# An earlier third second-stage call in a Fourier-mixing and cosine-MLP kernel, and one weight row over another queue

## The chip, the cores and the metric

The kernel runs on one core of a Trainium2 chip. The metric is the time of one execution on the device in microseconds (us); the kernel before has a median of 1911.01 us over three runs (1909.88 to 1911.72). Engines are named as in the profile: PE is TensorE's matmuls and PEld its weight loads, DVE is VectorE, ACT is ScalarE, POOL is GpSimd, SP is SyncE, which here only issues DMAs.

## The reference

```python
def _attn_ref(x):                      # x: 8 x 3008 x 256, float32
    X = np.fft.fft(x, axis=1)
    X = np.fft.fft(X, axis=2)
    return X.real.astype(np.float32)

def _moe_ref(x, w_in, w_out):          # 256 x 2048 and 2048 x 256
    h = x @ w_in
    g = h * np.cos(h)
    return (g @ w_out).astype(np.float32)
# the 24064 x 256 rows of the first are the x of the second
```

## The kernel before

The transform over the sequence is split as 3008 = 47 x 64. A **first stage** folds the input (x plus and minus its mirror) and multiplies it by cosines and sines of the 47; its result z goes to DRAM (`zd<-zs`) and comes back turned (`z<-zd`). A **second stage** multiplies z by the table `BJ` and gives `pq`, the input of the matmuls with `w_in`. The transform over the 256 columns is folded into `w_in` beforehand: `WC` and `WS` are the folded weights, and one row of each, `nrow`, is kept aside as a norm row. It has 2048 values, in four quarters of 512.

The main work is a list of 384 **steps**: 8 batches, 6 groups of sequence columns each (225 columns in group 0, 256 in the others), 8 steps a group. So batch b has the steps 48b to 48b+47. One step makes 2 x 128 hidden units for one group:

- `seed` (ACT, L734) writes the norm row's part, nb times a column of `wn`, into a PSUM tile H;
- `mm1(cur, 0)` (PE, L764, `WC`), `act_e` (ACT, L775), `mm1(cur, 1)` (PE, `WS`), `dve_h` (DVE, L780) make H and its partner h;
- `act_round` (ACT, L795), `dve_frac` (DVE, L799), `act_sin` (ACT, L805), `dve_g` (DVE, L809) make the cosine's argument, its sine and the product, once for H and once for h;
- `dve_s` (DVE, L820 and L830) makes sums S, and `mm2` (PE, L855) multiplies by `w_out` and its sums `VX`, adding into PSUM tiles M over the 8 steps of a group.

The steps are pipelined by hand in one loop. In pass t, PE does mm1 of step t and mm2 of step t-3; DVE does h of step t, the fractions of step t-1, g and S of step t-2 and the last S of step t-3; ACT seeds step t+1. After a group, ACT takes M (`take_m`, L876), GpSimd combines it (L907), DVE transposes it (L957) and SP stores it.

The next batch's transform runs beside the steps, in places that are written out as offsets. `transform(b)` counts from t0 = 48(b-1), the first step of the batch before. It puts loads of x, folds on GpSimd (`fold_rows`, L339; `fold_ends`, L351) and on DVE (`fold_pair`, `fold_edge`, L364) into passes, and **sessions** into the dictionary `sessions`: a session is a call whose matmuls stand between mm1(cur, 0) and mm2 of a pass. First-stage sessions (L396) are at t0 + 12, 20, 28 and 36. Second-stage sessions (`later_pair`, products L537) take two groups each: call 0 at t0 + 44, call 1 at t0 + 54, call 2 at t0 + 62. Their results go into a PSUM bank (`pb`) and into the H tile that step t+1 will use; ACT copies both into `pq` (`take_pair`, L584), and SP sends one row to DRAM and spreads it over the partitions as nb (L587, L588). Call 2 serves groups 4 and 5, whose first step is t0 + 80.

Batch 0 has its first stage and its groups 0 and 1 in an opening of its own; its calls 1 and 2 are at steps 14 and 22, and are needed at steps 16 and 32. The opening writes the queues out by hand: SP issues, in this order, the third quarter's columns of the norm row, a part of BJ, `send_row(3)` (the last quarter of the norm row to DRAM, `wd<-nrow`, L689), `take_columns(3)` (back as columns of `wn`, `wn<-wd`, L692, 512 elements of 4 bytes), `load_z(0, 1)` (L523), two loads of `w_out` (`load_w2`, L254), and then batch 1's x. GpSimd's queue has stores of z, four adds, three memsets, and then 14 loads of batch 1's x (L182) and two of its ends (L191); after them stand GpSimd's sums of `w_out` for the last four eighths (L907) and the first `fold_rows`. The last quarter of `wn` is first read by the seed of step 6, in pass 5.

In the loop the order around a session is:

```python
        if session:
            dve_g(old, 0)
            session[0](*session[2:], step(t + 1))
        if done and t > LAG:
            mm2(done, 0)
        if session:
            session[1](*session[2:], 1, step(t + 1).H)
```

Of the kernel before, what the change touches and what calls it, by code (L numbers as in the profile page):

```python
# [136 lines left out]
def kernel(  # L137
# [7 lines left out]
    nc = tc.nc  # L145
# [143 lines left out]
    nrow = {}  # L289
# [227 lines left out]
    def load_z(b, far):  # L517
        if b not in z2s:
            z2s[b] = spool.tile([128, NJ * 128], FP, tag="z2", bufs=1, name="z2")
        cols = slice(128 * JA, None) if far else slice(0, 128 * JA)  # L520
        zv = zds[b, far].rearrange("(x e r) c -> e x r c", e=2, r=2)
        for e in range(2):
            ins = nc.sync.dma_start(out=z2s[b][64 * e : 64 * e + 64, cols], in_=zv[e])  # L523
        return ins
# [83 lines left out]
    def transform(b):  # L608
        t0 = (b - 1) * NG * 8

        def at(o, *call):
            todo.setdefault(max(t0 + o, LAG - 1), []).append(call)

        for p, o in enumerate((0, 13) if b == 1 else (-20, -9)):
            for k in range(4):
                at(0 if o == 0 else o + k, load_later_x, b, p, k % 2, k // 2)
        at(0 if b == 1 else -16, load_ends, b)
        for c in range(NCH):
            o = 7 + 8 * (c // 2) + 2 * (c % 2)
            for e in range(2):  # L620
                aside.setdefault(t0 + o + e, []).append((fold_rows, b, c, e))
                between.setdefault(t0 + o + e + 1, []).append((fold_pair, c, e))
        for k in range(NCH // 2):
            o = 12 + 8 * k
            sessions[t0 + o] = first_half_later, take_half, b, k
            at(o, take_first, b, k)
            at(o + 1, store_z, b, k, 0)
            at(o + 1, store_z, b, k, 1)
        for e in range(2):
            o, f = (9 + e, 11) if b == 1 else (8 * e - 3, 6 + e)  # L630
            aside.setdefault(t0 + o, []).append((fold_ends, e))
            between.setdefault(t0 + f, []).append((fold_edge, e))
        at(38, load_z, b, 0)
        at(38, load_z, b, 1)
        later_pair(t0 + 44, b, 0)
        later_pair(t0 + 54, b, 1)
        later_pair(t0 + 62, b, 2)

    def later_pair(t, b, k):
        sessions[t] = second_pair, take_pair, b, k  # L640
        todo.setdefault(t, []).append((take_plus, b, k))
# [32 lines left out]
    def keep_row(e, n, pw, _):  # L674
        if n > 1:
            nrow[n] = half_tile("nrow", n)
        nc.vector.tensor_copy(out=nrow[n][0:1, :], in_=pw[0:1, :])
# [6 lines left out]

    wds = {}

    def send_row(n):
        wds[n] = dpool.tile([1, 512], FP, tag="wd", bufs=4, name="wd")
        nc.sync.dma_start(out=wds[n], in_=nrow[n][0:1, :])  # L689

    def take_columns(n):
        nc.sync.dma_start(  # L692
            out=wn[:, 4 * n : 4 * n + 4], in_=wds[n].rearrange("o (q p) -> (o p) q", p=128)
        )

# [326 lines left out]
    for row in range(2):  # L1022
        send_row(row)
    load_w2(0, 2)
    load_w2(2, 4)
    send_row(2)
    for k, c in enumerate(order[4:]):
        store_z(0, c, 1)
        if k:
            take_columns((1, 2, 0)[k - 1])  # L1030
# [11 lines left out]
        for dst, a, b, less in w2_sums:  # L1042
            aside.setdefault(f - 1, []).append((add, dst[:, f], a[:, f], b[:, f], less))
    n = len(steps)
    later_pair(14, 0, 1)
    later_pair(22, 0, 2)
    for b in range(1, NB):
        transform(b)

# [8 lines left out]
    clear_later(dve_h(s0))  # L1058
    late = fold_weights(1, 3, units=(1,), pw=late[2])
    keep_row(*late)  # L1060
    send_row(3)
    take_columns(3)
    load_z(0, 1)
    load_w2(4, 6)
    load_w2(6, 8)
# [136 lines left out]
```

## Time and profile before

| | |
|---|---|
| median of three runs | 1911.01 us |
| the profiled execution's own time | 1911.12 us |
| its span, first to last instruction | 1909.3 us |
| granted TensorE clock, mean | 0.999 |
| PE busy | 1894.7 us (99%) |
| DVE busy | 1781.9 us (93%) |
| ACT busy | 1489.5 us (78%) |
| POOL busy | 413.9 us (22%) |
| chain that ended last, by engine | PE 95%, DMA 2%, DVE 1% |

Times in a timeline count from the span's start. "Busy" is a union of an engine's instructions; matmuls are pipelined, so the end of one overlaps the start of the next. What stands in brackets at the end of a row is the idle time ahead of it and what ended it. A wait row reads: engine and line that waited, what it waited for, us in total, how often, the longest.

### The profile page before, as it was taken

What the parts mean: (1) busy time and instruction counts of PE and PEld (TensorE: products, weight loads), DVE (VectorE), ACT (ScalarE), POOL (GpSimd) and SP (SyncE); (2) the same over time, 40 slices, a digit from 0 to 9 for tenths busy, and PEclk for the clock granted to TensorE, in tenths of its full rate; (3) what the DMA queues carried; (4) which work ended last, traced back from release to release, by engine and by line L of the source; (5) the groups of instructions that cost most, each with busy time, mean ns of one, the idle gap of its engine ahead of it and who ended that gap; (6) DMA issues with size and microseconds to landing.
All of it is one profiled execution on the core that took longest, in us unless ns stands there. A gap on an engine that the chain in (4) does not pass through costs nothing.

```text
span 1909.3 us, 31666 instructions
## 1 busy us (share of the span) xinstructions
PE 1894.7 (99%) x10486; PEld 1664.4 (87%) x10486; DVE 1781.9 (93%) x3340; ACT 1489.5 (78%) x2682; POOL 413.9 (22%) x493
## 2 busy tenths in 40 slices
PE   8999999999999999999999999999999999999998
PEld 5888898888988889888898888988889888898887
DVE  7999999999999999999999999999999999999998
ACT  4777887778777887778877878778777877787775
POOL 5322112221122211222122221122211222111111
PEclk9999999999999999999999999999999999999999
DMA  7321311113111131111311113111231001200001
GB/s 221 79 56 44 72 51 26 30 47 74 42 33 28 50 75 35 35 32 45 80 33 32 28 46 91 27 26 28 54 86 26 24 20 29 59 20 16 13 22 23
DMA packets 154132, 88.61 MB, mean 46 GB/s; under 512 B 106207, under 2 KB 146058, under 8 KB 151629
## 3 DMA queue, kind: packets, MB, share of 16 engines
q1 hardware_dynamic: 150561, 82.80, 17.9%
q0 software_dynamic: 1376, 1.84, 0.4%
q10 hardware_dynamic: 2032, 1.95, 0.3%
q8 instruction: 83, 1.36, 0.3%
q14 instruction: 80, 0.66, 0.1%
HBM read 49.27 MB, written 37.28 MB: 45 GB/s over the span
## 4 chain that ended last, share of the span: by engine, by line
PE 95%; DMA 2%; DVE 1%; POOL 0%; issue 0%; ACT 0%; SPq 0%; ACTq 0%; DVEq 0%; POOLq 0%
PE M L855 59%; PE H L764 33%; PE pz L396 1%; PE pb L537 1%; DMA z<-zd 1%; DMA xp<-in_x_dram 0%; DVE S L820 0%; DVE r L809 0%; POOL zd L513 0%; PE pz L459 0%; PE H L537 0%; DVE S L830 0%; PE H L396 0%; DMA out_dram<-ob 0%; DVE xp L214 0%
## 5 line engine op out<-in xcount | busy, mean ns | idle before, releaser
L855 PE MATMUL M<-S,VX 128*128 128x256 f32 (+1 forms) x2304 | 612.3, 375 | 0.0
L855 PEld LDWEIGHTS M<-S,VX 128*128 128x128 f32 x2304 | 437.7, 190 | 50.0
L795 ACT ACTIVATE r<-H 128x512 f32<-128x512 f32 (+1 forms) x384 | 226.3, 589 | 284.9 <-DVE h L780 282.4
L805 ACT ACTIVATE r<-r 128x1024 f32<-128x1024 f32 (+1 forms) x384 | 395.9, 1031 | 28.8 <-DVE r L799 21.3
L855 PE MATMUL M<-r,w 128*128 128x256 f32 (+1 forms) x1536 | 393.4, 378 | 0.0
L764 PE MATMUL H<-pq,WS 128*128 128x256 f32 (+1 forms) x1536 | 388.0, 375 | 1.2 <-ACT ew L775 1.2
L764 PE MATMUL H<-pq,WC 128*128 128x256 f32 (+1 forms) x1536 | 387.7, 375 | 0.0
L734 ACT ACTIVATE H<-nb,wn 128x256 f32<-128x256 f32 (+1 forms) x762 | 362.0, 475 | 14.0
L780 DVE TENSOR_TENSOR h<-ew,H 128x512 f32<-128x512 f32 (+1 forms) x384 | 259.2, 675 | 90.3 <-PE H L764 72.0
L764 PEld LDWEIGHTS H<-pq,WS 128*128 128x128 f32 x1536 | 291.5, 190 | 35.8 <-ACT ew L775 2.9
L855 PEld LDWEIGHTS M<-r,w 128*128 128x128 f32 x1536 | 296.1, 196 | 27.4
L764 PEld LDWEIGHTS H<-pq,WC 128*128 128x128 f32 x1536 | 291.6, 190 | 31.2
L799 DVE SCALAR_TENSOR_TENSOR r<-r,H 128x512 f32<-128x512 f32 (+1 forms) x384 | 258.8, 674 | 18.3
L820 DVE TENSOR_TENSOR S<-r 128x512 f32<-128x512 f32 (+1 forms) x384 | 260.9, 679 | 0.1
L907 POOL TENSOR_TENSOR cb<-cb,mr 128x256 f32<-128x256 f32 (+3 forms) x190 | 159.2, 849 | 465.9 <-DVE S L830 313.5
L799 DVE SCALAR_TENSOR_TENSOR r<-r,h 128x512 f32<-128x512 f32 (+1 forms) x384 | 259.5, 676 | 0.0
L775 ACT ACTIVATE ew<-H 128x512 f32<-128x512 f32 (+1 forms) x384 | 225.9, 588 | 42.5 <-PE H L764 37.8
L809 DVE SCALAR_TENSOR_TENSOR r<-h,r 128x512 f32<-128x512 f32 (+1 forms) x384 | 258.5, 673 | 0.0
L809 DVE SCALAR_TENSOR_TENSOR r<-H,r 128x512 f32<-128x512 f32 (+1 forms) x384 | 256.7, 669 | 0.7 <-ACT r L805 0.2
L795 ACT ACTIVATE r<-h 128x512 f32<-128x512 f32 (+1 forms) x384 | 235.7, 614 | 0.0
L339 POOL TENSOR_TENSOR xs<-xp 113x512 f32<-113x512 f32 x112 | 143.0, 1277 | 419.1 <-DVE S L830 303.9
L855 PE MATMUL M<-S,w 128*128 128x256 f32 (+1 forms) x768 | 228.9, 380 | 2.9 <-DVE S L830 2.6
(113 smaller groups left out, 1534.5 us busy)
## 6 DMA issues: line engine op xcount, KB each, us to landing
out_dram<-ob SPq DMA_DIRECT2D x726, 32.0 KB
xp<-in_x_dram SPq DMA_DIRECT2D x256, 56.0 KB
z<-zd SPq DMA_DIRECT2D x16, 640.0 KB
zd<-zs SPq DMA_DIRECT2D x120, 80.0 KB
nb<-nd SPq DMA_DIRECT2D x23, 256.0 KB
xp<-in_x_dram SPq DMA_DIRECT2D x52, 48.0 KB
xp<-in_x_dram SPq DMA_DIRECT2D x42, 49.0 KB
z<-zd SPq DMA_DIRECT2D x16, 128.0 KB
```

What stands on the lines that cost most here:

```text
L339: return nc.gpsimd.tensor_tensor(out=rows_of(c, e)[0:XL], in0=xv[:, 0], in1=xv[:, 1], op=ALU.subtract if e else ALU.add,)
L734: nc.scalar.activation(out=s.H[:, u * T : u * T + T], in_=s.nb[:, 0:T], func=AF.Copy, bias=0.25, scale=wn[:, f : f + 1],)
L764: nc.tensor.matmul(s.H[:, u * T : u * T + T], lhsT=W[:, 128 * f : 128 * f + 128], rhs=s.pq[e][:, 0:T], start=False, stop=True, skip_group_ ...
L775: nc.scalar.mul(out=s.ew[:, 0 : 2 * s.T], in_=s.H[:, 0 : 2 * s.T], mul=2.0)
L780: return nc.vector.tensor_tensor(out=s.h[:, 0 : 2 * T].rearrange("p (u t) -> p u t", u=2)[:, :, ::-1], in0=s.ew[:, 0 : 2 * T].rearrange("p ...
L795: nc.scalar.activation(out=r, in_=h, func=AF.Copy, bias=BIG, scale=1.0)
L799: nc.vector.scalar_tensor_tensor(out=r, in0=r, scalar=-BIG, in1=h, op0=ALU.add, op1=ALU.subtract)
L805: nc.scalar.activation(out=r, in_=r, func=AF.Sin, bias=0.0, scale=SIN_SCALE)
L809: nc.vector.scalar_tensor_tensor(out=r, in0=h, scalar=-0.25, in1=r, op0=ALU.add, op1=ALU.mult)
L820: return nc.vector.tensor_tensor(out=sv[:, 0:2], in0=gv[:, 2:3].to_broadcast([128, 2, T]), in1=gv[:, 0:4:3], op=ALU.subtract,)
L855: nc.tensor.matmul(acc[key][m // 2][:, 256 * (m % 2) : 256 * (m % 2) + T], lhsT=w, rhs=a, start=first, stop=s.fp == 7, skip_group_check=True,)
L907: return nc.gpsimd.tensor_tensor(out=o, in0=a, in1=b, op=ALU.subtract if less else ALU.add)
```

## The change

Three edits. In every batch from 1 on, call 2 of the second stage goes from t0 + 62 to t0 + 57, which is from step 14 to step 9 of the batch itself, counted from its own first step. In batch 0, calls 1 and 2 go from steps 14 and 22 to steps 9 and 14. And the last quarter of the norm row and its columns are issued on GpSimd's queue instead of SP's; they stand there behind the memsets of `clear_later` and ahead of GpSimd's loads of batch 1's x. The number of instructions of each kind on TensorE, VectorE and ScalarE stays; two DMAs change their queue.

```diff
@@ transform(b)
         later_pair(t0 + 44, b, 0)
         later_pair(t0 + 54, b, 1)
-        later_pair(t0 + 62, b, 2)
+        later_pair(t0 + 57, b, 2)
@@
-    def send_row(n):
+    def send_row(n, queue=nc.sync):
         wds[n] = dpool.tile([1, 512], FP, tag="wd", bufs=4, name="wd")
-        nc.sync.dma_start(out=wds[n], in_=nrow[n][0:1, :])
-
-    def take_columns(n):
-        nc.sync.dma_start(
+        queue.dma_start(out=wds[n], in_=nrow[n][0:1, :])
+
+    def take_columns(n, queue=nc.sync):
+        queue.dma_start(
             out=wn[:, 4 * n : 4 * n + 4], in_=wds[n].rearrange("o (q p) -> (o p) q", p=128)
         )
@@
-    later_pair(14, 0, 1)
-    later_pair(22, 0, 2)
+    later_pair(9, 0, 1)
+    later_pair(14, 0, 2)
@@
     keep_row(*late)
-    send_row(3)
-    take_columns(3)
+    send_row(3, nc.gpsimd)
+    take_columns(3, nc.gpsimd)
     load_z(0, 1)
```

## The prediction

> **What bounds the kernel now.** I read the engine table first, then the length of every step in the TensorE timeline, then the waits of a stretch in which steps are long, then that stretch in the DVE and ACT timelines, and last the opening on the SP and POOL queues.
>
> ```profile
> PE 1894.7 (99%) x10486; PEld 1664.4 (87%) x10486; DVE 1781.9 (93%) x3340; ACT 1489.5 (78%) x2682; POOL 413.9 (22%) x493
> ```
>
> TensorE is the bound. A step lasts from its first `H<-pq,WC` matmul to the next one's; most full steps last 4.75 us, first-stage or second-stage calls included 6.04. So 99% can only shrink where a step is longer than its matmuls. I number steps within a batch, 0 to 47; step 57 of the diff is step 9 of a batch, 62 is 14. Steps 8 to 11 last 4.62, 4.56, 4.70 and 4.87 us in batch 3 (begun at 767.82, 772.44, 777.00, 781.70, ended 786.57) and the same within 0.01 in batches 2 to 6; in batch 7, which folds no next batch, they last 4.39, 4.39, 4.39 and 4.75 (from 1701.88). The matmuls are the same, so 0.23, 0.17, 0.30 and 0.13 us are stalls. The waits of batch 3's stretch 763.6 to 793 name them; batch 7's stretch has no such row:
>
> ```profile
> PEld M L855 <- DVE S L830: 0.9, 3, 0.4
> ```
>
> The three timelines of step 10 (start, us):
>
> ```profile
> 780.25 0.93 PE L855 MATMUL M<-S,VX 128*128 128x225 f32 x4
> 781.21 0.66 PE L855 MATMUL M<-S,w 128*128 128x225 f32 x2
> 781.70 1.03 PE L764 MATMUL H<-pq,WC 128*128 128x256 f32 x4
> ```
> ```profile
> 776.67 0.68 DVE L780 TENSOR_TENSOR h<-ew,H 128x512 f32<-128x512 f32 x1
> 777.27 0.69 DVE L809 SCALAR_TENSOR_TENSOR r<-H,r 128x512 f32<-128x512 f32 x1
> 778.02 0.69 DVE L799 SCALAR_TENSOR_TENSOR r<-r,H 128x512 f32<-128x512 f32 x1
> ...
> 780.43 0.42 DVE L364 TENSOR_TENSOR xf<-xs 113x254 f32<-113x254 f32 x1
> 780.76 0.39 DVE L830 TENSOR_TENSOR S<-r,S 128x225 f32<-128x225 f32 x1
> ...
> 781.40 0.69 DVE L780 TENSOR_TENSOR h<-ew,H 128x512 f32<-128x512 f32 x1
> ```
> ```profile
> 777.39 0.60 ACT L795 ACTIVATE r<-H 128x512 f32<-128x512 f32 x1 [1.02 <-DVE h L780]
> 782.12 0.60 ACT L795 ACTIVATE r<-H 128x512 f32<-128x512 f32 x1 [0.15 <-DVE h L780]
> ```
>
> DVE goes from one h (776.67) to the next (781.40) in 4.73 us without a pause, against 4.39 of matmuls: the fold (L364, 0.33 of it) is what batch 7 lacks. The last matmul pair waits for S of 780.76 and starts at 781.21, 0.05 us behind its end, where it could have started at 781.01. ACT rounds only once h is done, and DVE's L799 waits for that rounding: h, rounding, L799 is the loop.
>
> In the opening:
>
> ```profile
> 36.99 0.24 SPq L689 DMA_DIRECT2D wd<-nrow  x1
> 39.60 0.36 SPq L692 DMA_DIRECT2D wn<-wd  x1
> 40.18 1.24 SPq L523 DMA_DIRECT2D z<-zd  x2
> ```
> ```profile
> 53.96 0.27 PE L537 MATMUL M<-BJ,z 64*64 64x64 f32 x1 [0.28 <-DMA z<-zd]
> ```
> ```profile
> 67.16 1.70 DVE L820 TENSOR_TENSOR S<-r 128x450 f32<-128x450 f32 x1
> ```
>
> SP sits 2.3 us between the row and its columns, with z behind them, and TensorE later waits for z. The third line is an op that takes 0.62 us elsewhere: GpSimd's fold (66.99, 1.38 us) runs beside it.
>
> **Part 1, batches 1 to 7, third call from step 14 to 9.** Removed and added alike: 64 products on TensorE, two ACT copies (0.59, 0.58), two DMAs. A call lengthens a step by 1.30 us (6.05 against 4.75 at 14; 5.48 against 4.19 at 6), so TensorE's own sum is unchanged. What changes is when DVE gets 1.30 us to catch up. Walking batch 3 on, in us from a step's start: step 9 now needs 4.39+1.30 = 5.69. Its products need L809 on H, done at 0.89; the call at 14, which waits for nothing, starts its products at 0.96, so no new wait (at most 0.05). h must now wait for the longer step: 4.82 instead of 4.24. That is 0.87 before step 10, earlier 0.33: DVE gains 0.54. ACT's rounding starts at -0.15, L799 at 0.48 instead of 1.02; S for the last pair is ready at 3.61 instead of 4.15, the pair starts at 4.01 unhindered, and the 0.17 of step 9 and 0.30 of step 10 are gone. In step 10 ACT has an extra copy (0.47 start to start) ahead of its two M copies: it is busy until 4.66, so the next rounding starts 0.27 into step 11, not at 0.07 when h would allow it, and not at 0.42 as before. So DVE keeps 0.15 of the 0.54: S at 4.06 instead of 4.21, against the 4.17 that the pair can bear (it starts 0.15 behind S there, and is due at 4.32). The 0.13 of step 11 is gone, narrowly. Step 8 is ahead of the call and keeps 0.23; step 12's 6.15 is longer matmul work (it also does the ends), not a stall. Steps 14 to 19 lose their call; steps 22 to 27 already run transposes and folds that way, each at 4.75 to 4.81, so I put nothing there. Gain 0.60 a batch, batches 1 to 6: **3.6 us** (1.9 if ACT's copies give half of steps 10 and 11 back). Batch 7 has no stall to lose: 0. On SP the row and norms now go ahead of the z stores at 13; nobody reads them before step 32.
>
> **Part 2, batch 0, calls at 9 and 14.** Excess over batch 7 in steps 9 to 11: 0.17, 0.35, 0.62 (two more folds in 11, 0.20 each). The same walk removes the first two; in 11 S comes 0.15 sooner, so 0.15 of 0.62. **0.7 us** (0.2 to 1.1). The call at 9 needs BJ's columns, issued at 62.59; it reads them near 71, and they have to be there: the nearest row, POOL's wait ended by the loads of that time, ends at 66.99. SP now waits at step 9 for ACT's copy, with ident and seven x loads behind it (63.06 to 69.5 before, now to about 81); the folds that read them come at step 23, near 130.
>
> **Part 3, the row and columns on GpSimd's queue.** Removed from SP: two issues (0.24, 0.36) and the 2.3 us wait. z is issued 2 to 2.9 us earlier, and w2 and the x loads behind it. The wait for z costs 1.23 us (53.35 to 54.58) less 0.63 (half a call): **0.6 us** (0 to 0.6; GpSimd's x loads, now behind the columns, compete less with z). The Trainium skill, "DMA: Bandwidth & Descriptors", Issuing engines are not separate DMA queues, says that issuing from another engine saves only issue time; by it z would gain 0.6 us of start and TensorE perhaps none. The row contradicts that reading, since what leaves SP is a wait for a landing.
>
> Earlier w2 and x loads shift GpSimd's adds (57.21, held 12.14 us by w2) and its first fold (66.99, held by loads) against DVE. Batch 0's steps 7 and 8 last 5.13 and 5.61 against 4.19 and 4.39: 2.2 us lost beside them. Three us earlier, the adds meet DVE's idle 1.2 and 0.9 us of step 6. I take **0.5 us** off, between -1 and 2. The skill's "SBUF — State Buffer", Who interferes with whom, calls this an exclusive lock for whichever starts first; the 1.70 us row agrees.
>
> On POOL, 14 x loads and two xz loads are now behind a wait for the row's landing (2.6 us on SP; POOL's zd issues took 6.1) and two more issues, 3 to 7 us in all: POOL is then done issuing near 49 to 52, still ahead of the w2 that its adds wait for. The columns are issued at 40 to 43 and were 5 us in flight on SP at most; they are read by ACT's seed of step 6 at 50.73. Cost taken 0, cover 2 us or more.
>
> **Sum.** 3.6+0.7+0.6+0.5 = 5.4 us off the profiled execution's own 1911.12 (span 1909.3), which is 0.1 above the median: 1905.7, or **1905.6** as a median.
>
> **Rivals.** *ACT gives it back* (0.24): the extra copies put off the rounding of steps 10 and 11 and GpSimd's adds meet DVE elsewhere. For it: rounding in step 11 waited for h by only 0.15. Against: the walk has it earlier by 0.15. Gain 1.9+0.2+0 = 2.1: 1908.9. *Late columns, slower* (0.06): the wn columns are 512 elements of 4 bytes, and POOL's loads issued at 43 took 12 us to land. If row and columns need 6 and 19 us, they land near 62; ACT waits 11 us at the seed of step 6, DVE's slack there is 0.6 plus the 2.1 idle of step 6, so 8.7 are lost and 4.9 gained: 1914.9. It decides from a landing past 58, and 53 before it costs anything. Against: 5 us on SP in the same traffic. *The forecast* (0.70).
>
> **Numbers.** Best ends 3.6+1.1+0.6+2 = 7.3, worst of the first two cases 1.9+0.2-1 = 1.1; with the 0.9 us of spread in the runs shown, 1902.8 to 1909.8. A change of 0.2% (3.8 us) is what a measurement of this kernel can tell: faster means below 1907.2. Faster 0.70, within 0.24, slower 0.06.
>
> **What would show it.** Batches 1 to 6: step 9 at 5.69, 10 at 4.39, 11 at 4.75, 14 at 4.75. If 10 or 11 stays long with ACT's L795 no longer waiting for h, ACT is the rival. z ahead of TensorE in step 5 shows part 3; an ACT wait on wn at 50.7 the slow one. Wrong altogether if step 9 exceeds 5.8 or steps 14 to 19 grow.

## The result

The changed kernel takes 1905.63 us (median of 7 runs, 1904.71 to 1905.90) against 1911.01 for the kernel before (7 runs, 1909.71 to 1912.26): a ratio of 0.9971, 95% interval 0.9960 to 0.9983. The forecast was 1905.6. On another chip, later, the two stood at 1904.99 and 1911.81, 0.9967 (0.9955 to 0.9980). The profiled execution took 1905.63 with a span of 1903.9 (before 1911.12 and 1909.3).

The engine table of the kernel after, to be held against the PE, PEld, DVE, ACT and POOL line of before:

```profile
PE 1890.0 (99%) x10486; PEld 1668.0 (88%) x10486; DVE 1783.2 (94%) x3340; ACT 1486.8 (78%) x2682; POOL 416.1 (22%) x495
```

The counts are the same but for POOL's two DMAs. PE's busy time is 4.7 us shorter with the same matmuls, because this table counts most of the waits as busy: the pair that waited for S in step 10 of before stands at 781.21, only 0.03 behind the modelled end of the row ahead of it (780.25 and 0.93). Where the time went is read from the step lengths (start of the first `H<-pq,WC` matmul to the next one, in the TensorE timelines), us:

| | before | after |
|---|---|---|
| batches 2 to 6, step 8 | 4.62 | 4.62 |
| step 9 | 4.57 | 5.77 |
| step 10 | 4.70 | 4.39 |
| step 11 | 4.87 | 4.75 |
| step 14 | 6.04 | 4.75 |
| batches 1 to 6, all steps | 1401.16 | 1398.01 |
| batch 0, step 5 | 5.50 | 4.91 |
| steps 7 and 8 | 10.74 | 10.42 |
| steps 9, 10, 11 | 4.56, 4.74, 5.37 | 5.76, 4.39, 5.14 |
| step 22 | 6.04 | 4.75 |
| batch 0, all steps | 235.12 | 233.52 |
| batch 7, all steps | 221.27 | 221.27 |
| ahead of step 0 | 29.76 | 29.39 |
| from the start of the last step on | 22.05 | 21.67 |

So 3.15 come from batches 1 to 6, 1.60 from batch 0, 0.37 lie ahead of the first step and 0.38 behind the last: 5.5, which is the difference between the two profiled times (1911.12 and 1905.63).

The wait row of batch 3's stretch, 763 to 800 (the same waits had 0.9 us in three, at most 0.4):

```profile
PEld M L855 <- DVE S L830: 0.3, 1, 0.3
```

One is left, step 8's, ahead of the moved call. The steps 9 to 11 of batch 3 in the three timelines of the kernel after (step 9 starts at 769.42, 10 at 775.19, 11 at 779.58):

```profile
769.42 1.03 PE L764 MATMUL H<-pq,WC 128*128 128x256 f32 x4
770.38 0.27 PE L537 MATMUL pb<-BJ,z 64*64 64x64 f32 x1
770.46 0.24 PE L537 MATMUL H<-BJ,z 64*64 64x64 f32 x1
...
779.20 0.55 PE L855 MATMUL M<-S,w 128*128 128x225 f32 x2
779.58 1.03 PE L764 MATMUL H<-pq,WC 128*128 128x256 f32 x4
```
```profile
769.70 0.61 DVE L809 SCALAR_TENSOR_TENSOR r<-H,r 128x450 f32<-128x450 f32 x1
...
774.31 0.69 DVE L780 TENSOR_TENSOR h<-ew,H 128x512 f32<-128x512 f32 x1 [0.57 <-ACT r L805]
...
775.66 0.69 DVE L799 SCALAR_TENSOR_TENSOR r<-r,H 128x512 f32<-128x512 f32 x1
...
778.41 0.38 DVE L830 TENSOR_TENSOR S<-r,S 128x225 f32<-128x225 f32 x1
...
783.20 0.42 DVE L830 TENSOR_TENSOR S<-r,S 128x256 f32<-128x256 f32 x1
```
```profile
775.03 0.60 ACT L795 ACTIVATE r<-H 128x512 f32<-128x512 f32 x1 [0.79 <-DVE h L780]
...
776.05 0.58 ACT L584 COPY pq<-pb 128x512 f32<-128x512 f32 x1
...
779.84 0.59 ACT L795 ACTIVATE r<-H 128x512 f32<-128x512 f32 x1
```

In these steps, where DVE had no pause before, one row has a bracket: DVE ran dry for 0.57 us ahead of h of 774.31, so it is no longer behind. That h stands 0.88 ahead of step 10 (before 0.33). S of step 10 is done at 778.79, its pair starts 0.41 us later (before 0.05) and goes at its own pace (0.55 us, not 0.66). In step 11 the rounding (779.84) has no bracket and starts 0.11 behind the end of h (779.05 and 0.68), where 0.03 was enough in step 10: ACT, not h, sets it.

### The profile page after: what moved, and what is told of

The parts are those of the page before. It is cut to its first block, busy times and chain, and to the rows that moved or that the text cites. A ratio compares the mean times of both kernels' runs of the same rounds, so it can differ in the third digit from the quotient of the medians.

```text
span 1903.9 us, 31661 instructions
## 1 busy us (share of the span) xinstructions
PE 1890.0 (99%) x10486; PEld 1668.0 (88%) x10486; DVE 1783.2 (94%) x3340; ACT 1486.8 (78%) x2682; POOL 416.1 (22%) x495
## 4 chain that ended last, share of the span: by engine, by line
PE 97%; DVE 1%; DMA 1%; issue 0%; ACT 0%; SPq 0%; ACTq 0%; DVEq 0%
PE M L855 59%; PE H L764 34%; PE pz L396 1%; PE pb L537 1%; PE H L537 0%; DMA xp<-in_x_dram 0%; DVE r L799 0%; DVE r L809 0%; PE pz L459 0%; DVE S L820 0%; DVE S L830 0%; DMA z<-zd 0%; PE H L396 0%; DMA out_dram<-ob 0%; DVE xp L214 0%
## 5 line engine op out<-in xcount | busy, mean ns | idle before, releaser
L799 DVE SCALAR_TENSOR_TENSOR r<-r,H 128x512 f32<-128x512 f32 (+1 forms) x384 | 258.7, 674 | 18.9 <-ACT r L795 0.4
L820 DVE TENSOR_TENSOR S<-r 128x512 f32<-128x512 f32 (+1 forms) x384 | 259.8, 677 | 0.1
L799 DVE SCALAR_TENSOR_TENSOR r<-r,h 128x512 f32<-128x512 f32 (+1 forms) x384 | 259.4, 675 | 0.0
L809 DVE SCALAR_TENSOR_TENSOR r<-h,r 128x512 f32<-128x512 f32 (+1 forms) x384 | 259.0, 675 | 0.0
L809 DVE SCALAR_TENSOR_TENSOR r<-H,r 128x512 f32<-128x512 f32 (+1 forms) x384 | 255.7, 666 | 0.6 <-ACT r L805 0.2
```

The costliest lines, as they stand in the source:

```text
L799: nc.vector.scalar_tensor_tensor(out=r, in0=r, scalar=-BIG, in1=h, op0=ALU.add, op1=ALU.subtract)
L809: nc.vector.scalar_tensor_tensor(out=r, in0=h, scalar=-0.25, in1=r, op0=ALU.add, op1=ALU.mult)
L820: return nc.vector.tensor_tensor(out=sv[:, 0:2], in0=gv[:, 2:3].to_broadcast([128, 2, T]), in1=gv[:, 0:4:3], op=ALU.subtract,)
```

## The experiments

Lengths of steps are those of the table's kind. In the variants with one line more in the code, L809, L820 and L830 are called L810, L821 and L831.

**The three parts by themselves, and another order on SP.** The first has only the third call of batches 1 on at step 9:

```diff
-        later_pair(t0 + 62, b, 2)
+        later_pair(t0 + 57, b, 2)     # the kernel before, with this alone
```

> The kernel before with one number changed: the third call of batches 1 to 6 (and 7) at step 9 of a batch instead of 14; batch 0's calls and the queues as before. Theory (DVE, 4.73 us of work against 4.39 of matmuls in steps 8 to 11, gets the call's 1.30 us of cover before steps 10 and 11): in every batch from 1 to 6 step 9 goes from 4.57 to 5.77, step 10 from 4.70 to 4.39, step 11 from 4.87 to 4.75, step 14 from 6.05 to 4.75; 0.52 us a batch, 3.1 us in all, batch 0 and the opening unchanged; time about 1907.9. Rival (those batches gain because the opening starts earlier, or ACT's extra copies need the other edits): steps 10 and 11 stay over 4.6 and 4.85, under 1.5 us in all. The z wait of 1.23 us in step 5 of batch 0 stays in both.

Measured 1907.66 (11 runs; before on the same chip 1910.78): 0.9984, interval 0.9975 to 0.9993. Batches 1 to 6 take 5.77, 4.39, 4.75 and 4.75 in steps 9, 10, 11, 14 and 1398.03 us in all, as in the kernel after; steps 9 to 11 of batch 0 stay. The call's move alone makes those 3.1 us. Unforeseen: step 0 began 1.1 us earlier here than in the profile of before, and 0.75 of that went into a longer wait for z (step 5 took 6.25).

The second has batch 0's calls alone:

```diff
-    later_pair(14, 0, 1)
-    later_pair(22, 0, 2)
+    later_pair(9, 0, 1)               # the kernel before, with these alone
+    later_pair(14, 0, 2)
```

> The kernel before with batch 0's two calls alone moved, from steps 14 and 22 to 9 and 14; the rest as before. Theory: step 9 about 1.20 longer, 10 about 0.35 shorter, 11 about 0.2 shorter, 22 1.30 shorter, net 0.6 to 0.7 us off; step 5 keeps its wait for z, steps 7 and 8 stay at 5.13 and 5.61; batches 1 to 6 unchanged within 0.05. Rival (the shorter step 11 comes from GpSimd's fold being shifted by the queue edit, not from the call): 10 and 11 stay at 4.74 and 5.37, net 0 to 0.2.

Measured, one execution: 1908.92 (before on the same chip 1910.78); steps 9, 10, 11 and 22 at 5.77, 4.39, 5.13 and 4.75, so 1.21 more and 0.35, 0.24 and 1.29 less: 0.67 off, by the calls and not by the queue. The rest of the distance is not the edit's: step 5 had 6.38, and steps 7 and 8 together 10.01 instead of 10.74, though nothing before step 9 was edited. TensorE's first product of the opening's second stage in these two kernels, the one with the third call alone first:

```profile
53.62 0.27 PE L537 MATMUL M<-BJ,z 64*64 64x64 f32 x1 [1.03 <-DMA z<-zd]
```
```profile
53.12 0.27 PE L537 MATMUL M<-BJ,z 64*64 64x64 f32 x1 [1.16 <-DMA z<-zd]
```

The product stood at 53.96 in the profile of before. Step 0 began at 29.76, 28.67 and 28.04 in the three: a spread of 1.72, of which 0.84 is left at the product. The wait for z swallows half of an early start.

The third has the queue edit alone, with one execution first and a timed comparison after it:

```diff
-        later_pair(t0 + 57, b, 2)
+        later_pair(t0 + 62, b, 2)     # the kernel after, calls put back
...
-    later_pair(9, 0, 1)
-    later_pair(14, 0, 2)
+    later_pair(14, 0, 1)
+    later_pair(22, 0, 2)
```

> The kernel after with all calls back at their old steps, so that only the row and its columns on GpSimd's queue are left. Theory: step 5 of batch 0 0.6 shorter (no wait for z), steps 7 and 8 together 0.3 shorter, batches 1 to 6 unchanged: 0.9 us off, time about 1910. POOL waits some 4.5 us for the columns' landing behind its first x loads and issues xz only near 55. Rival (the start and the tail, each 0.4 us shorter in the run of the changed kernel, belong to the queue edit too): a further 0.4 in the time ahead of step 0, as a steady difference; by the theory that start differs from run to run and may as well be longer here.

The one execution took 1908.58. Step 5 was at 4.91 with a start at 28.05, so the gain there against a kernel with the same start (6.38) is 1.47, against the profile of before 0.59. The other half of the theory missed: steps 7 and 8 took 10.89, longer than before. The start is scatter (28.05 here, 29.83 below with the same code). The end is not: from the last step's start on it takes 21.67 to 21.70 in the eight profiles with the queue edit and 22.05 to 22.08 in the five without, a steady 0.38. There the rival was right. The trace shows what makes it. At the end SP waits for nine completion counters of the DMAs in a fixed order, 0.06 us each where nothing is to be waited for. The last landing comes 20.8 us behind the last step's start in all thirteen profiles (20.76 to 20.81). Without the queue edit it ends the third of the nine waits, and six more follow; with two DMAs fewer on SP's queue it ends the ninth, and none follows.

> The queue edit alone once more, now timed, because the time ahead of step 0 differs by up to 1.9 us from look to look and one look can't give its worth. Theory: TensorE's wait for z ends at a landing that hardly moves with that start, so the edit is worth 0.6 us where the program starts late and 1.5 where it starts early, and 0.38 at the end (the time behind the last step's begin is 21.67 to 21.69 with the edit, 22.04 to 22.08 without); steps 7 and 8 differ by as much among runs without the edit as between with and without, so nothing is put there: 1.0 to 1.9 us off. Rival (contention in steps 7 and 8 takes it back): under 0.6 off, steps 7 and 8 at 10.9 or more again.

Measured 1908.62 (11 runs) against 1911.81: 0.9985, interval 0.9977 to 0.9994, so 2.9 us off by the ratio, between 1.1 and 4.4 (3.2 between the medians). The estimate of 1.0 to 1.9 lies in the interval's lower part; the rival is out. Steps 7 and 8 were at 10.43 this time. The opening agrees with the lower part: step 6 starts at 53.18 on average over the eight profiles with the edit and at 54.08 over the four without it and without the order below, 0.90 earlier, though the eight began 0.38 later on average (28.96 against 28.58). Counted from step 0, step 6 comes after 24.22 us in all eight, within 0.01, and after 24.82 to 25.93 in the four (25.51 on average): 1.29, with the 0.38 at the end 1.7. Whether the 2.9 is more than that, the interval doesn't decide.

The fourth keeps SP for everything and puts z ahead of the columns:

```diff
     send_row(3)
-    take_columns(3)
     load_z(0, 1)
+    take_columns(3)                   # the kernel before, with this order
```

> The kernel before with two lines in another order on SP's queue: z goes ahead of the columns of the last norm row; nothing goes to GpSimd's queue, and no call is moved. Theory (what leaves SP is the wait for the row's landing, whoever's queue takes it): z is issued 2 us or more earlier and step 5 loses its 0.6 us as with the queue edit; POOL's xz is issued near 45 as before and its adds start when w2 has landed, some 2.5 us earlier than 55.2. Steps 7 and 8 then go by where the adds fall: between 0.5 better and 1 worse than before. The columns land some 2 us later than before, and ACT's seed of step 6 waits for them for at most 1 us. Rival (z gains because GpSimd's loads are held back by its wait, so that z lands in less traffic): z lands later than 53.3 and step 5 keeps over half of its wait.

Measured, one execution: 1912.43, above all 15 runs of before on that chip (1909.14 to 1911.89); one execution decides little by itself, but its steps do. SP, ACT and TensorE in its opening:

```profile
37.69 1.64 SPq L523 DMA_DIRECT2D z<-zd  x2
40.70 0.37 SPq L692 DMA_DIRECT2D wn<-wd  x1
```
```profile
54.86 0.94 ACT L734 ACTIVATE H<-nb,wn 128x225 f32<-128x225 f32 x2 [4.49 <-DMA wn<-wd]
```
```profile
55.85 1.65 PE L764 MATMUL H<-pq,WC 128*128 128x225 f32 x4 [2.27 <-ACT H L734]
```

z came in time, as the theory has it: the first product stands at 52.89 without a wait, and the rival is out. But the 2 KB of columns, issued behind 1280 KB of z, landed 14 us later; ACT's seed of step 6, due at 50.4, sat until 54.86 where "at most 1 us" was expected, and TensorE followed. Against the timed profile of the queue edit, steps 5 and 6 took 7.25 and 6.40 instead of 4.91 and 4.76, 4.0 lost; 1.3 came back in steps 7 and 8 (9.15 against 10.43), and batch 0 as a whole was 2.6 longer (236.88 against 234.24; before 235.12). GpSimd missed its expectation too: its loads waited for earlier landings, the last was issued at 52.58 instead of near 45, and its adds started at 56.47, behind the 55.2 that they were to come ahead of by 2.5. This is the mechanism of the slower rival, "late columns", in another kernel. It also shows what the other queue bought: in the kernel after the columns went out at 38.99 and landed 8.5 us later by the profile's table of issues.

**Whether DVE's sum is the bound.**

```diff
-                between.setdefault(t0 + o + e + 1, []).append((fold_pair, c, e))
+                between.setdefault(t0 + o + e + 1, []).append((fold_pair, c, e, b < 3))
...                                    # where the last value is false, fold_cols leaves out DVE's part
```

> The kernel before, leaving out VectorE's fold (L364, 113x254, 0.33 to 0.42 us) for the transforms of batches 3 to 7, so done in batches 2 to 6; ACT's copies of the fold, the calls (the third at step 14) and the queues stay. Theory (DVE's sum bounds steps 8 to 11): batches 2 to 6 take batch 7's lengths, 4.39, 4.39, 4.39 and 4.75, with the call still at 14: 0.83 us a batch, 4.1 us in all; batches 0 and 1 as before. Rival (ACT's copies or GpSimd's fold make those steps long, and the call at 9 helps by putting ACT's copies elsewhere): batches 2 to 6 keep 4.62, 4.56, 4.70 and 4.87 or lose less than half of the excess.

Measured: 4.39, 4.39, 4.39 and 4.75 in steps 8 to 11 of batches 2 to 6, with the call still at 14, and batch 1 unchanged; batches 2 to 6 became 4.5 us shorter, 1906.09 in one execution. (Most of the 0.4 above the estimate is batch 4's, outside these steps.) DVE's timeline of batch 3, step 10:

```profile
774.55 0.68 DVE L781 TENSOR_TENSOR h<-ew,H 128x512 f32<-128x512 f32 x1
...
778.31 0.39 DVE L831 TENSOR_TENSOR S<-r,S 128x225 f32<-128x225 f32 x1
...
778.95 0.68 DVE L781 TENSOR_TENSOR h<-ew,H 128x512 f32<-128x512 f32 x1
```

From h to h 4.40 us instead of 4.73, which is the matmuls' 4.39 within 0.01. ACT and GpSimd have as many instructions as before (2682 and 493), and the stalls are gone; they were DVE's 0.33 over.

**Where the call has to stand.**

```diff
-        later_pair(t0 + 57, b, 2)
+        later_pair(t0 + 58, b, 2)     # the kernel after; and t0 + 66
```

> The kernel after with the third call of batches 1 to 7 one step later, at step 10. Theory (what counts is that DVE gets 1.30 us ahead of the stalled pairs): step 9 back to 4.57 (its stall of 0.17 comes ahead of the call), step 10 at 5.69 to 5.77 (the call's 1.30 on 4.39, with at most 0.08 for the H tile that L809 still reads), step 11 at 4.75: 0.17 less what the smaller wait gives back, so batches 1 to 6 0.6 to 1.0 us longer in all than with the call at 9. Rival (ACT, whose two M copies of step 10 and two of the call now fall into one step, sets steps 10 and 11): step 10 over 5.8 or step 11 over 4.85, and 2 us or more lost.

Measured, one execution: 1907.48. Step 9 4.57, step 10 5.83, step 11 4.75; batches 1 to 6 took 1399.44, 1.43 more than with the call at 9. The 0.17 of step 9 came back as expected, but the loss is above the expected 0.6 to 1.0, because step 10 is 0.14 over 5.69, not 0.08. It is also over the 5.8 that the rival named; step 11 and the loss stay within its bounds. DVE and TensorE in batch 3's step 10, which starts at 774.88:

```profile
775.14 0.68 DVE L809 SCALAR_TENSOR_TENSOR r<-H,r 128x512 f32<-128x512 f32 x1
```
```profile
775.83 0.33 PE L537 MATMUL pb<-BJ,z 64*64 64x64 f32 x2
775.98 0.24 PE L537 MATMUL H<-BJ,z 64*64 64x64 f32 x1
```

The call's second half writes the H tile that this L809 reads. L809 ends at 775.82, H's first product starts at 775.98, 1.10 into the step where 0.96 is usual: all of the 0.14, so it is this wait and not ACT. The L809 of this step works on 512 columns (0.68 us), that of step 9 on 450 (0.61).

> The kernel after with the third call of batches 1 to 7 at step 18 of a batch, nine steps later. Theory: the call is no cost wherever it lies, only its cover for DVE counts, so batches 1 to 6 go back to 4.62, 4.56, 4.70 and 4.87 in steps 8 to 11, step 14 stays at 4.75 and step 18 takes 6.04: 0.52 us a batch, 3.1 us longer in all than after. Rival (step 14 was a poor place in itself, beside the transposes and folds, and any other is better): steps 9 to 11 long but step 18 below 5.9, half or more of the 3.1 us kept.

Measured, one execution: 1907.70. Steps 8 to 11 at 4.62, 4.57, 4.70 and 4.87, step 14 at 4.75, step 18 at 6.07; 3.3 us more than in the kernel after over batches 1 to 6, all of the gain. The wait row of the same stretch is that of before, word for word:

```profile
PEld M L855 <- DVE S L830: 0.9, 3, 0.4
```

So the call costs much the same in the four places tried (1.30 at step 14, 1.32 at 18, at 9 and 10 the 1.30 and the wait for H's tile), and is worth something only ahead of steps in which DVE is behind.

**The next step in the same direction.** One fold of DVE goes from the step ahead of the call into the call's own:

```diff
-                between.setdefault(t0 + o + e + 1, []).append((fold_pair, c, e))
+                f = o + e + 1 + (c == e == 0)
+                between.setdefault(t0 + f, []).append((fold_pair, c, e))
```

> The kernel after with the first of four folds of each next batch (the fold_pair of c = 0, e = 0) moved from step 8 to step 9 of a batch, the one that now has the call. Theory (DVE is still 0.33 us over in step 8, and that makes step 8 long by 0.23 and lets the read of H by L809 end 0.15 too late for the call's products in step 9): step 8 goes from 4.62 to 4.39, step 9 from 5.77 to 5.69 to 5.72, steps 10 and 11 keep 4.39 and 4.75: 0.28 to 0.30 us a batch in batches 2 to 6, a little in 0 and 1, 1.5 to 2.0 us in all, time about 1904.0. Rival (the slack that the call gives DVE is used up by its present folds, as the 0.02 us of margin in step 11 suggests): step 10 or 11 grows by 0.15 or more, and the net is under 0.6 us either way.

Measured 1902.58 (5 runs), 0.9952 of before (0.9938 to 0.9966). A second time, beside the kernel after on the same chip:

> The changed kernel with the first fold moved from step 8 to 9, beside the changed kernel on the same chip. Theory: batches 1 to 6 are 1.8 us shorter in all (0.30 to 0.33 a batch) and the rest differs only by the scatter of start and of steps 7 and 8, so 1.5 to 2.5 us below the changed kernel. Rival (the first run's 1902.58 owed its distance to an early start of 28.35 and short steps 7 and 8): within 1 us of the changed kernel.

> The changed kernel again, beside its fold variant and the queue edit alone on one chip. Theory: 5.0 to 5.6 us below the kernel before (3.1 from batches 1 to 6, 0.65 from batch 0's calls, 1.0 to 1.9 from the queue edit). Rival (the sum of the parts overstates, since parts share a wait): under 4.5 below.

Measured 1903.13 (5 runs) beside 1904.99 for the kernel after (5 runs) and 1911.81 before: 0.9954 (0.9941 to 0.9968) and 0.9967 (0.9955 to 0.9980). The medians are 1.86 apart, as the theory has it; the two intervals overlap, and the steps decide: 8 to 11 of batches 2 to 6 take 4.39, 5.69, 4.39 and 4.75 in both profiles, 1.84 us less over batches 1 to 6. The rival is out. Batch 3 of the second, DVE and TensorE:

```profile
768.77 0.61 DVE L810 SCALAR_TENSOR_TENSOR r<-H,r 128x450 f32<-128x450 f32 x1
...
771.80 0.75 DVE L364 TENSOR_TENSOR xf<-xs 113x254 f32<-113x254 f32 x2
...
773.42 0.69 DVE L781 TENSOR_TENSOR h<-ew,H 128x512 f32<-128x512 f32 x1 [0.27 <-ACT r L806]
```
```profile
769.56 0.27 PE L537 MATMUL pb<-BJ,z 64*64 64x64 f32 x1
769.57 0.27 PE L537 MATMUL H<-BJ,z 64*64 64x64 f32 x1
```

Two folds now stand in step 9 (0.75) and DVE still runs dry for 0.27 before the next h. L810 ends at 769.38, 0.18 before the call wants H, so both halves of the call start together. This is the fastest version of the study: in batches 2 to 6 it has no stall left in these steps (batch 1's step 9 still takes 5.76), and batches 2, 5 and 6 take the 232.59 us of the kernel without folds. The kernel after itself stands 6.8 us below before on this chip by medians, above the 5.0 to 5.6 expected, which lie inside the interval (3.8 to 8.6).

## Why the prediction was right

The stalls, what made them and what the moved call does to them were forecast rightly. That the time came within 0.1 us is luck: errors cancel, and the measurement itself leaves some 2 us either way (0.9960 to 0.9983).

*Batches 1 to 6, 3.6 forecast, 3.15 measured.* The walk held term by term, times from a step's start: h 0.87 ahead of step 10 (0.88 measured), its fraction at 0.48 (0.47, L799 at 775.66), its S at 3.61 (3.60), ACT's rounding of step 11 at 0.27 (0.26), S of step 11 at 4.06 (783.20 and 0.42, so 4.04); steps 10, 11 and 14 at 4.39, 4.75 and 4.75, steps 15 to 19 not longer. The term that was wrong is "no new wait (at most 0.05)". L809 ends at 770.31, 0.89 into step 9 as forecast, but H's first product stands at 770.46, 0.15 behind it. The walk had taken 0.07 for that hand-over, from nothing but the products' usual start at 0.96; its own 0.15 between S and the pair of step 11 would have given the 0.08. Step 9 is 5.77 instead of 5.69: 0.08 a batch, all of the shortfall of 0.45. The variant with one fold less in step 8 lets L810 end 0.18 before the call and takes the 0.08 away; the variant at step 10 nearly doubles it.

*Batch 7, 0:* measured 0. *Batch 0, 0.7:* measured 0.67, with the calls alone too. Here as well two misses cancel: step 9 took 5.76, not 5.69, and step 11 gave back 0.23 of its excess (5.14), not 0.15.

*The wait for z, 0.6:* 0.59 between the two profiles. But it was taken from one start of the program. The profiles of the variants show starts from 27.84 to 29.83, and without the edit an early start turns into a wait, so the edit is worth up to 1.7 (step 5 took 6.61 in the variant without folds, which began at 27.84, against 4.91). The z loads went out at 38.03 instead of 40.18. By "Issuing engines are not separate DMA queues" in the Trainium skill's "DMA: Bandwidth & Descriptors" only the issue time should be saved; the trace differs, since a wait for a landing left SP's queue along with the two issues (0.60 of the 2.15 us). The order experiment adds that getting rid of that wait on the same queue is a loss if the small load then goes behind the large one.

*Contention, 0.5:* not shown. Steps 7 and 8 are 0.32 shorter between the two profiles, but with no edit ahead of them they took 10.74, 10.38, 10.01 and 10.93 in the four profiles of the old opening, and between 9.73 and 10.89 in the eight with the queue edit. The term read one draw of a spread of 1.2 us as a quantity. The bounds of -1 to 2 were the honest part of it.

*The columns, 0:* right in outcome, with a wrong step in between. POOL's queue and ACT's seed in the kernel after:

```profile
35.81 0.53 POOL L689 DMA_DIRECT2D wd<-nrow  x1
38.99 0.82 POOL L692 DMA_DIRECT2D wn<-wd  x1 [2.65 <-DMA wd<-nrow]
39.80 3.53 POOL L182 DMA_DIRECT2D xp<-in_x_dram  x7
47.79 0.50 POOL L182 DMA_DIRECT2D xp<-in_x_dram  x1 [4.46 <-DMA wn<-wd]
...
55.17 1.06 POOL L907 TENSOR_TENSOR VX<-w 128x128 f32<-128x128 f32 x2
```
```profile
50.37 0.94 ACT L734 ACTIVATE H<-nb,wn 128x225 f32<-128x225 f32 x2
```

The columns landed 8.5 us behind 38.99, at 47.5, 2.9 ahead of the seed, which has no bracket: the cover of 2 us or more held. The row's landing held POOL 2.65 (2.6 forecast). But the step "3 to 7 us in all" was short: POOL finished issuing at 55.15 instead of 45.07, 10.1 later, because the eighth load behind the columns waited another 4.46 for them, and two later ones 2.4 in all for earlier loads. The forecast had POOL done by 49 to 52, ahead of the w2 loads; in fact GpSimd's adds now start right behind POOL's own queue, without a wait for w2. They start 2.0 earlier than before all the same, so nothing was lost.

*The rivals.* "ACT gives it back" fell at step 11: ACT does set the rounding, as the forecast said too, and S still meets its pair. "Late columns" was real as a mechanism and priced too low: the order experiment, with a landing near 54.8, lost 2.6 where the rival's own slack (0.6 and 2.1 off a wait of 4.5) gives 1.8. That kernel has none of the calls' gains, so the landing past 58, from which the rival has the changed kernel slower than before, was not tried. In the changed kernel the landing came 2.9 us ahead of the seed, and 5.5 ahead of the 53 from which the rival counted a cost.

*Not forecast:* the 0.38 at the program's end, and 0.37 of a start that scatters. Together with the short 0.45 and the 0.2 of contention they explain why the sum fits.

*Sums that don't come out.* Half of the 0.30 and 0.13 given back leaves 2.3 us in batches 1 to 6, not 1.9. The late columns' 11 us less 0.6 and 2.1 is 8.3 lost, not 8.7. The range's upper end of 1909.8 is the first rival's 1908.9 and the spread; from the worst case of 1.1 that stands beside it, it would be 1910.8. None of the three touches the forecast.

## What to carry to other kernels

A block of work on the bounding engine that costs the same anywhere is a tool: put it just ahead of the steps in which a second engine is behind by a little each time, and then move that engine's own extra work into the same step. Where a moved block writes a buffer that another engine still reads, take the hand-over from a row in which it waits, not from one in which it doesn't. And before pricing a term in the opening, ask how much it differs between executions of the same code; an early start only passes through if no fixed landing stands behind it.

## What the runs showed of the hardware that was not expected

- TensorE's first product into a tile that DVE still reads starts 0.15 to 0.16 us behind the end of DVE's instruction (770.31 to 770.46, 775.82 to 775.98). Where a pair waits for S as its input, it started 0.06 behind it in step 10 of before (781.15 to 781.21) and 0.15 in step 11 (785.91 to 786.06), so one figure doesn't serve for all.
- GpSimd's DMAs rotate over eight completion counters in this program; the eighth load behind the columns carries the columns' counter, and waited 4.46 us in the kernel after and 5.07 in the queue edit's first profile for their landing, though it needs nothing of them. A slow 2 KB transfer blocked a queue of 48 and 56 KB loads.
- 2 KB in pieces of 4 bytes took 8.5 and 9.1 us on GpSimd's queue (the same two profiles) and 14 on SP's behind 1280 KB. On SP ahead of z, in the kernel before, the packets of 4 bytes moved within 4 us of the issue at 39.60 (40.5 to 43.5). Behind z they began at 45.0, when most of z's packets had started, some 300 moved by 46.5, and the others only from 49 to 54, among the 1 KB packets of w2: of the 14 us, some 4 went by behind z and 10 beside the next loads.
- The end of this program was 0.38 us longer where the counter of the last landing stood third of nine in SP's closing waits than where it stood ninth: six waits of 0.06.
- Beside GpSimd's first fold in the kernel after, DVE's instruction with both inputs in SBUF is long, and the one ahead of it, with one input in PSUM, is not:

```profile
64.73 1.28 POOL L339 TENSOR_TENSOR xs<-xp 113x512 f32<-113x512 f32 x1 [0.22 <-DVE r L809]
```
```profile
64.80 0.62 DVE L799 SCALAR_TENSOR_TENSOR r<-r,H 128x450 f32<-128x450 f32 x1
65.34 1.15 DVE L809 SCALAR_TENSOR_TENSOR r<-h,r 128x450 f32<-128x450 f32 x1
```

  L809 ends at 66.49, 0.48 behind the fold's end at 66.01; alone it takes 0.62 in this group. The Trainium skill's "SBUF — State Buffer", Who interferes with whom, says that two SBUF inputs contend with GpSimd's reads and one does not; these rows agree.
